# Attention into routed experts on one core: token rows by transposes, gate logits in column groups, another order of a pair's matmuls

## The chip, the cores and the metric

The kernel runs on one NeuronCore of a Trainium2 chip. The metric is the device time of one execution in microseconds (us), the median of three runs. A difference of 0.3% is 3.0 us.

## The reference

Three stages, all in float32. Attention with a sigmoid in place of the softmax, on 4 batches (b) of 12 heads, 448 tokens and head size 64; then a mixture of 8 experts, where each of the 1792 tokens goes to the expert with the largest gate logit; then a dense two-layer block. Cut to what matters:

```
scores = q @ k.T / 8 - log(448)
attn   = sigmoid(scores) @ v                 # [4, 12, 448, 64]
x      = attn as [1792 tokens, 768]
logits = x @ w_gate                          # [1792, 8]
e      = argmax(logits);  gate = softmax(logits)[e]
x      = gate * (relu(x @ w1[e]) @ w2[e])
out    = relu(x @ w_in)**2 @ w_out
```

The argmax makes the logits delicate: they are computed in full float32, where TensorE makes two passes of each matmul (two records in the trace).

## The kernel before, in words

The change lies in the attention stage, lines 130 to 289. It works through 24 units: a unit is a pair of heads, (b, j) with j from 0 to 5, so that the pair's 128 output features are the columns 128j to 128j+127 of x. The loop over units (from line 259) writes out by hand the order in which every engine gets its instructions; within one engine the order of the program is kept. It is a pipeline over units: in iteration n the scores of unit n are computed, the products with v of unit n-1, and the token rows of unit n-2.

TensorE's 128x128 array is used in three forms. In the **row form** the array is cut into two halves of 64 rows: `score` (L181) for c = 0, 1, 2 computes 128 keys of both heads side by side, one head in each half, as three passes of a split into a rounded and a rest part (L168, L169 on DVE make the parts). In the **column form** it is cut into halves of 64 columns: `av` (L191) for c = 0, 1, 2 multiplies v with the attention of both heads side by side. In the **full form** the whole array is used: `score` for c = 3 (L183, the last 64 keys of both heads), `av` for c = 3 (L194), and `rows` (L204).

In one iteration TensorE gets, in this order: score 0 and 1 of unit n (row form), av 0 and 1 of unit n-1 (column form), score 2 (row form), score 3, av 3 and rows (full form), av 2 (column form). Scores go through ACT (the sigmoid, L185) into tiles `a`. The four av steps of a unit accumulate in one bank `po`, and `fin_av` (L198, DVE) copies it to `xT`, features by tokens.

`rows` (L200 to 212) turns xT of a unit into token rows and also gives the unit's share of the gate logits: for each of four chunks of 112 tokens it multiplies xT (stationary) with `iw`, the identity of 128 columns beside the 8 gate columns of this j: 136 moving columns, two passes, 8 passes a unit. ACT copies the result to `xn` (L206), a DMA on ACT's queue writes the rows to `x_d`, and DVE adds the 8 logit columns to `lg` (L210, L212). After the last unit the routing begins with a maximum over `lg` on DVE (L335).

Beside this DVE and ACT convert the weights of the dense block, two iterations to a chunk of weights (`convert`, lines 226 to 243; its operations are L106, L108, L111, L113 on DVE and L109 on ACT). In an iteration DVE gets, in this order: the split of the unit after the next score (L168, L169), the first half of the conversion, the logits' add, the copy to xT, the second half of the conversion. So behind the copy to xT there stand, in DVE's queue, a conversion step of half the chunk and the split of the next iteration. SP's queue holds the loads of q, k, v (L160, L161) and of raw weights (L95); POOL's queue holds the writes of converted weights (L115, L125).

PSUM is full: two banks of `po`, two of `pt`, four of score tiles.

Of the kernel before, what the change touches and what calls it, by code (L numbers as in the profile page):

```python
# [10 lines left out]
F32 = mybir.dt.float32  # L11
# [5 lines left out]
AF = mybir.ActivationFunctionType  # L17
ALU = mybir.AluOpType
AX = mybir.AxisListType

B, H, S, D = 4, 12, 448, 64
NT = B * S
DM = H * D
E = 8
# [2 lines left out]
NP = H // 2  # L27
CP = 112
NC = S // CP
KD = DM // 128  # L30
KF = FF // 128
KF2 = FF2 // 128
NR = B * NC
IW = 128 + E
NTL = NT // 128
NSLOT = NTL + E - 1
NBASE = NTL + 1
# [24 lines left out]
def moe_kernel(ctx: ExitStack, tc: tile.TileContext, qk, v, wg, wm, w2, out):  # L62
    nc = tc.nc
# [6 lines left out]
    x_d = dram.tile([NT + 128, DM], F32, name="x_d")  # L70
# [5 lines left out]
    ident = const.tile([128, 128], F32, name="ident")  # L76
# [57 lines left out]
    with ExitStack() as actx:  # L134
        xp = actx.enter_context(tc.tile_pool(name="xp", bufs=1, reuse_waits="tile"))
        sp_ = actx.enter_context(tc.tile_pool(name="sp_", bufs=2, reuse_waits="tile"))
        ps_a = actx.enter_context(tc.tile_pool(name="ps_a", bufs=2, space=PS, reuse_waits="tile"))
        wctx = actx.enter_context(ExitStack())
        ps_e = actx.enter_context(tc.tile_pool(name="ps_e", bufs=1, space=PS, reuse_waits="tile"))
# [2 lines left out]
        ap_ = wctx.enter_context(tc.tile_pool(name="ap_", bufs=6, reuse_waits="tile"))  # L142

        xT = {}
        iw = xp.tile([128, KD, IW], F32, name="iw")
        lg = xp.tile([CP, NR, E], F32, name="lg")
        for j in range(KD):
            nc.gpsimd.tensor_copy(iw[:, j, :128], ident)
        zero = xp.tile([128, DM // 8], F32, name="zero")
        nc.gpsimd.memset(zero, 0.0)  # L150

# [12 lines left out]
        def split_qk(n):  # L164
            r = loaded[n][0]
            rh = sp_.tile([128, QW], F32R, tag="qkh", name=f"qkh{n}")
            rl = sp_.tile([128, QW], F32R, tag="qkl", name=f"qkl{n}")
            nc.vector.tensor_copy(rh, r)  # L168
            nc.vector.tensor_tensor(rl, r, f32(rh), op=ALU.subtract)  # L169
            return [(rh, rh), (rh, rl), (rl, rh)]  # L170

        def score(b, j, c, terms):
            ps = ps_s.tile([128, 2, 512], F32, tag="sc", name=f"sc_{b}_{j}_{c}")
            o = S + 128 * c
            n = 2 if c < 3 else 1
            for i, (kp, qp) in enumerate(terms):
                flags = dict(start=(i == 0), stop=(i == len(terms) - 1), skip_group_check=True)
                if c < 3:
                    for h in range(2):
                        p = slice(64 * h, 64 * h + 64)  # L180
                        nc.tensor.matmul(ps[:, h, :S], kp[p, o:o + 128], qp[p, :S], **flags)  # L181
                else:
                    nc.tensor.matmul(ps[:, 0, :S], kp[:, o:o + 128], qp[:, :S], **flags)  # L183
            a = ap_.tile([128, 2, S], F32, tag="a", name=f"a_{b}_{j}_{c}", bufs=9)
            nc.scalar.activation(a[:, :n], ps[:, :n, :S], AF.Sigmoid, bias=bias_s, scale=1.0 / math.sqrt(D))  # L185
            return a

        def av(b, j, c, a, vr, po):
            if c < 3:
                for h in range(2):  # L190
                    nc.tensor.matmul(po[64 * h:64 * h + 64, :S], vr[:, 128 * c + 64 * h:128 * c + 64 * h + 64], a[:, h],  # L191
                                     start=(c == 0), stop=(c == 2), skip_group_check=True)
            else:
                nc.tensor.matmul(po[:, :S], vr[:, 384:512], a[:, 0], start=False, stop=False, skip_group_check=True)  # L194

        def fin_av(b, j, po):
            xT[b, j] = xp.tile([128, S], F32, tag="xT", name=f"xT_{b}_{j}", bufs=3)
            nc.vector.tensor_copy(xT[b, j], po[:, :S])  # L198

        def rows(b, j):  # L200
            pt = ps_e.tile([128, 2, 512], F32, tag="pt", name=f"pt_{b}_{j}")
            xn = sp_.tile([128, NC, IW], F32, tag="xn", name=f"xn_{b}_{j}")
            for c in range(NC):
                nc.tensor.matmul(pt[:CP, c // 2, (c % 2) * IW:(c % 2) * IW + IW], xT[b, j][:, c * CP:(c + 1) * CP], iw[:, j, :],  # L204
                                 start=True, stop=True, skip_group_check=True)
            nc.scalar.activation(xn[:CP].rearrange("p (a c) n -> p a (c n)", a=2), pt[:CP, :, :2 * IW], AF.Copy)  # L206
            nc.scalar.dma_start(out=x_d[128 + b * S:128 + (b + 1) * S, j * 128:(j + 1) * 128].rearrange("(c p) d -> p c d", p=CP), in_=xn[:CP, :, :128])
            l = lg[:, b * NC:(b + 1) * NC, :]
            if j == 0:
                nc.vector.tensor_copy(l, xn[:CP, :, 128:])  # L210
            else:
                nc.vector.tensor_tensor(l, l, xn[:CP, :, 128:], op=ALU.add)  # L212

        units = [(b, j) for b in range(B) for j in range(NP)]
        loaded = {n: load(*units[n]) for n in range(3)}
        done = []
        rawb, raw = [], []

        def extras():
            rows(*done.pop(0))  # L220
# [5 lines left out]
        def convert(n, half):  # L226
            if n < 2:
                if half == 0:
                    fetch(n)
                return  # L230
            m, o = divmod(n - 2, 2)
            if m < 0 or m >= PRE:
                return
            if o == 0 and half == 0:
                conv[m] = (conv[m], cvp.tile([128, 2 * CH if m >= 8 else CH], F32, tag="dst", name=f"cd{m}"),
                           cvp.tile([128, CH], F32, tag="ab", name=f"ca{m}", bufs=1))
            narrow(m, 1 + 2 * o + half, *conv[m])
            if o == 1 and half == 0 and m + 2 < PRE:
                fetch(m + 2)
            if o and half:  # L240
                narrow(m, 5, *conv[m])
            if (m == PRE - 1 if o and half else o == 0 and half == 0 and m > 0):
                last = m if o else m - 1
                narrow(last, 6, *conv.pop(last))

        def fetch(m):
            conv[m] = cvp.tile([128, 2 * CH], F32, tag="src", name=f"cs{m}")
            narrow(m, 0, conv[m], None, None)

        def av_step(c):  # L250
            if prev is not None:
                b, j, parts_, vr, po = prev
                av(b, j, c, parts_[c], vr, po)
                if c == 2:
                    fin_av(b, j, po)
                    done.append((b, j))

        terms = {0: [(loaded[0][0], loaded[0][0])]}
        for n, (b, j) in enumerate(units):
            if n + 3 < len(units):  # L260
                loaded[n + 3] = load(*units[n + 3])
            if n == 0:
                nc.sync.dma_start(out=iw[:, :, 128:], in_=wg)
                nc.sync.dma_start(out=x_d[0:128, :].rearrange("p (a n) -> p a n", a=8), in_=zero.unsqueeze(1).to_broadcast([128, 8, DM // 8]))
            if n >= len(units) - 4:
                rawb.append(rawp.tile([128, 2 * CH], F32, tag="raw", name=f"raw{n}", bufs=4))
                raw.extend([rawb[-1][:, :CH], rawb[-1][:, CH:]])
            vr = loaded.pop(n)[1]
            if n + 1 < len(units):
                terms[n + 1] = split_qk(n + 1)  # L270
            r = terms.pop(n)
            po = ps_a.tile([128, 512], F32, tag="po", name=f"po_{b}_{j}")
            cur = [score(b, j, 0, r), score(b, j, 1, r)]
            av_step(0)
            av_step(1)
            convert(n, 0)
            cur.append(score(b, j, 2, r))
            cur.append(score(b, j, 3, r))
            av_step(3)
            if done:  # L280
                extras()
            av_step(2)
            convert(n, 1)
            prev = (b, j, cur, vr, po)
        extras()
        for c in (0, 1, 3, 2):
            av_step(c)
        extras()
        wctx.close()

# [16 lines left out]
        m, me, es, g, gr, pos = (rt([CP, NR], n) for n in ("m", "me", "es", "g", "gr", "pos"))  # L307
# [151 lines left out]
    def trans_y(bi, h, t, yn, yT, pool, tags):  # L459
# [5 lines left out]
        for i in range(2):  # L465
            pt = pool.tile([128, 4, 128], F32, tag=tags[i], name=f"pyt_{bi}_{h}_{t}_{i}")
            js = range(i * per, min(KD, (i + 1) * per))
            for j in js:
# [16 lines left out]
    with ExitStack() as mctx:  # L485
# [19 lines left out]
        def xtrans(s, xg):  # L505
            xh = mp.tile([128, KD, 128], F32R, tag="xh", name=f"xh_{s}", bufs=1)
            xl = mp.tile([128, KD, 128], F32R, tag="xl", name=f"xl_{s}", bufs=1)
            for i, (j0, n) in enumerate(((0, 4), (4, 2))):
# [34 lines left out]
        def make_slot(s, xh, xl, weights):  # L543
# [14 lines left out]
            def up(c):  # L558
# [4 lines left out]
                for q in range(3):  # L563
# [3 lines left out]
                    o = q * 512  # L567
                    mm3(ps[i], xh[:, k, :], xl[:, k, :], w[:, o:o + 512], wl_[:, o:o + 512], k == 0, k == KD - 1)
                if c % 2 == 1:
# [270 lines left out]
    for bi, (t0, P) in enumerate(blocks):  # L840
# [65 lines left out]
        po = {}  # L906
# [30 lines left out]
        for o in range(len(PRODS)):  # L937
            for q in range(4):
                g = 4 * o + q
# [24 lines left out]
                if ty and g >= 20 and g - 20 < len(ty):  # L964
                    i = g - 20
# [59 lines left out]
```

## Time and profile before

| | |
|---|---|
| median of 3 runs | 995.42 us (994.38 to 997.09) |
| profiled execution, its time | 997.18 us |
| profiled execution, its span | 995.7 us |
| TensorE (PE) busy | 948.8 us, 95% |
| DVE, ACT busy | 637.6 us, 565.8 us |
| mean granted clock of PE | 0.976 of full speed |
| attention stage | to about 186 us |

The span is from the first to the last instruction of the profiled execution. PE is its matmuls, PEld its weight loads. In a timeline, each row is a run of like instructions of one line; the time of the last one includes the way through the array, so that consecutive rows overlap a little, and the distance from one start to the next tells what a step costs. A bracket behind a row tells how long the engine was idle before it, and what ended that.

### The profile page before, as it was taken

The numbers are of one execution on the slowest core, as the hardware profiler recorded it, in microseconds if no ns is written. First come the engines' busy times: TensorE is split into PE (matmuls) and PEld (weight loads), VectorE is DVE, ScalarE is ACT, GpSimd is POOL, SyncE is SP. The second block draws the span as 40 slices with busy tenths as digits, with TensorE's granted clock in tenths as the row PEclk, the third lists the DMA queues.
The fourth block names the chain that finished last, engine by engine and source line by source line (L and its number), as shares of the span: only waits on it lengthen the run. The fifth ranks groups of instructions, "written<-read, shape, count | busy, mean of one in ns | idle before, by whom it ended". The sixth has DMA issues, their size and how long they took to land. (4 is left out here: it accounts for less than half of the span.)

```text
span 995.7 us, 15057 instructions
## 1 busy us (share of the span) xinstructions
PE 948.8 (95%) x5870; PEld 799.4 (80%) x5870; DVE 637.6 (64%) x671; ACT 565.8 (57%) x674; POOL 144.1 (14%) x120
## 2 busy tenths in 40 slices
PE   7999999458999999999998999999999999999996
PEld 3555555247888888888887888889999999999996
DVE  2777779678777776777764467617776722228763
ACT  5666666265777777777774544536544434446540
POOL 0000000145513233421330000000000110000002
PEclk9999999777999999999999999999999999999998
DMA  8798887552496876359465164443334541223412
GB/s 289 245 322 288 291 296 255 190 239 79 136 384 213 312 280 223 128 196 360 160 235 188 29 260 184 153 164 95 96 96 143 183 150 64 64 65 96 127 32 95
DMA packets 51261, 184.32 MB, mean 185 GB/s; under 512 B 7856, under 2 KB 18736, under 8 KB 49136
## 3 DMA queue, kind: packets, MB, share of 16 engines
q1 hardware_dynamic: 33136, 146.48, 42.0%
q0 software_dynamic: 6832, 31.07, 8.0%
q10 hardware_dynamic: 11216, 5.75, 2.3%
q8 instruction: 47, 0.77, 0.3%
q14 instruction: 30, 0.25, 0.1%
HBM read 209.62 MB, written 36.97 MB: 248 GB/s over the span
## 5 line engine op out<-in xcount | busy, mean ns | idle before, releaser
L397 DVE TENSOR_TENSOR wl<-raw,wh 128x1536 fp32r<-128x1536 f32 x103 | 203.2, 1981 | 70.1 <-ACT wh L396 67.3
L396 ACT ACTIVATE wh<-raw 128x1536 fp32r<-128x1536 f32 x120 | 177.8, 1488 | 14.3 <-DMA raw<-in_wm 6.9
L185 ACT ACTIVATE a<-sc,bias_s 128x896 f32<-128x896 f32 x96 | 82.4, 908 | 36.0 <-PE sc L181 35.7
L864 ACT ACTIVATE r<-pp 128x512 f32<-128x512 f32 (+1 forms) x64 | 34.8, 544 | 111.5 <-PE pp L860 111.5
L956 PE MATMUL pq<-wrh,sh 128*128 128x384 f32 x264 | 89.1, 337 | 0.3 <-DVE raw L917 0.3
L958 PE MATMUL pq<-wrh,sl 128*128 128x384 f32 x264 | 88.7, 336 | 0.0
L957 PE MATMUL pq<-wrl,sh 128*128 128x384 f32 x264 | 88.7, 336 | 0.0
L527 PE MATMUL py<-wl,hh 128*128 128x384 f32 x240 | 82.8, 345 | 5.5 <-POOL wl L397 5.5
L526 PE MATMUL py<-wh,hh 128*128 128x384 f32 x240 | 86.3, 360 | 0.0
L528 PE MATMUL py<-wh,hl 128*128 128x384 f32 x240 | 83.0, 346 | 2.5 <-DVE hl L556 2.5
L397 POOL TENSOR_TENSOR wl<-raw,wh 128x1536 fp32r<-128x1536 f32 x17 | 60.0, 3534 | 161.4 <-ACT wh L396 161.4
L526 PE MATMUL ph<-wh,xh 128*128 128x512 f32 x180 | 76.0, 422 | 0.3 <-ACT xh L512 0.3
L397 DVE TENSOR_TENSOR wrl<-raw,wrh 128x1536 fp32r<-128x1536 f32 x30 | 52.7, 1757 | 35.8 <-ACT wrh L396 35.8
L527 PE MATMUL ph<-wl,xh 128*128 128x512 f32 x180 | 71.8, 399 | 0.0
L396 ACT ACTIVATE wrh<-raw 128x1536 fp32r<-128x1536 f32 x30 | 44.6, 1487 | 47.8 <-PE pq L958 43.0
L528 PE MATMUL ph<-wh,xl 128*128 128x512 f32 x180 | 71.7, 399 | 0.0
L872 DVE TENSOR_TENSOR h<-h,h 128x512 f32<-128x512 f32 (+1 forms) x16 | 10.0, 625 | 89.9 <-ACT h L867 89.9
L885 DVE TENSOR_TENSOR sl<-h,sh 128x1024 fp32r<-128x1024 f32 (+1 forms) x56 | 59.8, 1085 | 8.5 <-ACT sh L884 8.4
L191 PE MATMUL po<-a,qkv 128*64 128x448 f32 x288 | 64.7, 556 | 0.0
L832 POOL DMA_INDIRECT out<-raw,idx x14 | 13.7, 976 | 331.5 <-DVE raw L917 302.8
L884 ACT ACTIVATE sh<-h 128x1024 fp32r<-128x1024 f32 (+1 forms) x56 | 51.5, 943 | 13.5 <-PE pq L957 8.0
L858 PE MATMUL pp<-why,wrh 128*128 128x512 f32 (+1 forms) x132 | 48.9, 370 | 3.0 <-PEq L788 3.0
(235 smaller groups left out, 2188.3 us busy)
## 6 DMA issues: line engine op xcount, KB each, us to landing
raw<-in_wm SPq DMA_DIRECT2D x120, 768.0 KB
qraw<-in_wm SPq DMA_DIRECT2D x32, 768.0 KB
raw<-t_d SPq DMA_DIRECT2D x28, 768.0 KB
cs<-in_w SPq DMA_DIRECT2D x11, 1536.0 KB
raw<-w_d SPq DMA_DIRECT2D x16, 768.0 KB
qkv<-in_qk SPq DMA_DIRECT2D x23, 480.0 KB
raw<-in_w SPq DMA_DIRECT2D x5, 1536.0 KB
t_d<-raw POOLq DMA_DIRECT2D x5, 1536.0 KB, 7.7
```

Of the source, the lines that this page charges most:

```text
L185: nc.scalar.activation(a[:, :n], ps[:, :n, :S], AF.Sigmoid, bias=bias_s, scale=1.0 / math.sqrt(D))
L191: nc.tensor.matmul(po[64 * h:64 * h + 64, :S], vr[:, 128 * c + 64 * h:128 * c + 64 * h + 64], a[:, h], start=(c == 0), stop=(c == 2), skip ...
L396: nc.scalar.activation(h, src, AF.Copy)
L397: (nc.gpsimd if pool else nc.vector).tensor_tensor(l, src, f32(h), op=ALU.subtract)
L526: nc.tensor.matmul(ps, lh, rh, start=first, stop=False)
L527: nc.tensor.matmul(ps, lh, rl, start=False, stop=False)
L528: nc.tensor.matmul(ps, ll, rh, start=False, stop=last)
L884: nc.scalar.activation(sh[:, :2 * N], src, AF.Copy)
L885: V.tensor_tensor(sl[:, :2 * N], src, f32(sh[:, :2 * N]), op=ALU.subtract)
L956: nc.tensor.matmul(po[p][:, :DH], lh, wc[:, w0:w0 + DH], start=(q == 0 and kk == 0 and o in (0, 2, 5)), stop=False, **fl)
L957: nc.tensor.matmul(po[p][:, :DH], lh, wcl[:, w0:w0 + DH], start=False, stop=False, **fl)
L958: nc.tensor.matmul(po[p][:, :DH], ll, wc[:, w0:w0 + DH], start=False, stop=(q == 3 and kk == 1), **fl)
```

## The change

Three things. First, `rows` no longer multiplies with the identity beside the gate columns but uses TensorE's transpose with the identity: four instructions of 128 moving columns, one pass each. `pt` shrinks to one bank. Second, the gate logits are computed apart, by a new function `logits`: when j is 2 or 5 it multiplies the gate columns of three units (8 columns padded with zeros to 32, stationary) with their xT (448 moving columns), each unit in a group of 32 columns of the array of its own, into the freed bank `lgT`. When j is 5, the sums of the batch are complete: DVE copies 96 partitions of 448 columns to `ls`, four small matmuls with `pick` (8 moving columns) add the three groups and turn them into token rows, and DVE copies these to `lg`. `logits` is called right after score 0 and 1, and three more tiles of xT must live so long (5 buffers instead of 3). Third, the order within an iteration: score 0 and 1 (row form), the logits where due (column groups of 32), av 0, 1 and 2 (column form), score 2 (row form), score 3, rows and av 3 (full form). At the end of the stage: the rows of the last unit but one, av 0 to 3, the logits, the rows of the last unit.

```diff
+GW = 32
+GJ = 3
-IW = 128 + E
...
-        iw = xp.tile([128, KD, IW], F32, name="iw")
+        gw = xp.tile([128, KD, GW], F32, name="gw")
+        pick = xp.tile([128, E], F32, name="pick")
         lg = xp.tile([CP, NR, E], F32, name="lg")
-        for j in range(KD):
-            nc.gpsimd.tensor_copy(iw[:, j, :128], ident)
+        nc.gpsimd.memset(gw, 0.0)
+        nc.gpsimd.tensor_tensor(pick, ident[:, 0:E], ident[:, GW:GW + E], op=ALU.add)
+        nc.gpsimd.tensor_tensor(pick, pick, ident[:, 2 * GW:2 * GW + E], op=ALU.add)
...
-            xT[b, j] = xp.tile([128, S], F32, tag="xT", name=f"xT_{b}_{j}", bufs=3)
+            xT[b, j] = xp.tile([128, S], F32, tag="xT", name=f"xT_{b}_{j}", bufs=5)
             nc.vector.tensor_copy(xT[b, j], po[:, :S])
+        lgT = {}
+        def logits(b, j):
+            if j % GJ < GJ - 1:
+                return
+            if j == GJ - 1:
+                lgT[b] = ps_e.tile([128, 512], F32, tag="lgT", name=f"lgT_{b}")
+            for g in range(GJ):
+                i = j + 1 - GJ + g
+                nc.tensor.matmul(lgT[b][GW * g:GW * g + GW, :S], gw[:, i, :], xT[b, i], start=(i == g), stop=(i != g),
+                                 skip_group_check=True, tile_position=(0, GW * g))
+            if j < KD - 1:
+                return
+            ls = xp.tile([128, S], F32, tag="ls", name=f"ls_{b}", bufs=1)
+            nc.vector.tensor_copy(ls[:GJ * GW], lgT[b][:GJ * GW, :S])
+            o = lgT[b][:CP, S:S + NC * E].rearrange("p (c e) -> p c e", c=NC)
+            for c in range(NC):
+                nc.tensor.matmul(o[:, c], ls[:GJ * GW, c * CP:(c + 1) * CP], pick[:GJ * GW], start=True, stop=True, skip_group_check=True)
+            nc.vector.tensor_copy(lg[:, b * NC:(b + 1) * NC, :], o)
         def rows(b, j):
-            pt = ps_e.tile([128, 2, 512], F32, tag="pt", name=f"pt_{b}_{j}")
-            xn = sp_.tile([128, NC, IW], F32, tag="xn", name=f"xn_{b}_{j}")
+            pt = ps_e.tile([128, NC, 128], F32, tag="pt", name=f"pt_{b}_{j}")
+            xn = sp_.tile([128, NC, 128], F32, tag="xn", name=f"xn_{b}_{j}")
             for c in range(NC):
-                nc.tensor.matmul(pt[:CP, c // 2, (c % 2) * IW:(c % 2) * IW + IW], xT[b, j][:, c * CP:(c + 1) * CP], iw[:, j, :],
-                                 start=True, stop=True, skip_group_check=True)
-            nc.scalar.activation(xn[:CP].rearrange("p (a c) n -> p a (c n)", a=2), pt[:CP, :, :2 * IW], AF.Copy)
+                nc.tensor.transpose(pt[:CP, c], xT[b, j][:, c * CP:(c + 1) * CP], ident)
+            nc.scalar.activation(xn[:CP], pt[:CP], AF.Copy)
-            l = lg[:, b * NC:(b + 1) * NC, :]
-            if j == 0:
-                nc.vector.tensor_copy(l, xn[:CP, :, 128:])
-            else:
-                nc.vector.tensor_tensor(l, l, xn[:CP, :, 128:], op=ALU.add)
...
             if n == 0:
-                nc.sync.dma_start(out=iw[:, :, 128:], in_=wg)
+                nc.sync.dma_start(out=gw[:, :, :E], in_=wg)
...
             cur = [score(b, j, 0, r), score(b, j, 1, r)]
+            if done:
+                logits(*done[0])
             av_step(0)
             av_step(1)
+            av_step(2)
             convert(n, 0)
             cur.append(score(b, j, 2, r))
             cur.append(score(b, j, 3, r))
-            av_step(3)
             if done:
                 extras()
-            av_step(2)
+            av_step(3)
             convert(n, 1)
             prev = (b, j, cur, vr, po)
         extras()
-        for c in (0, 1, 3, 2):
+        for c in range(4):
             av_step(c)
+        logits(*done[0])
         extras()
```

`extras` is the call of `rows` for the oldest finished unit. `av_step(3)` now calls `fin_av`, where `av_step(2)` did.

## Rows read from the trace of the kernel before

**Rows 1.** Page, granted clock of PE in 40 slices of the span, in tenths.

```profile
PEclk9999999777999999999999999999999999999998
```

**Rows 2.** Windows, attention: stretch, length, busy us by engine, granted clock, DMA share, GB/s.

```profile
100.00:150.00 50.00, 50.00 (x301) 28.62 (x297) 37.93 (x43) 32.93 (x39) 1.60 (x3) 1.00 0.84 291
```

**Rows 3.** Timeline of PE over one iteration: start us, us, line, tiles, count.

```profile
126.78 0.47 PE L181 MATMUL sc<-qkh 64*128 64x448 f32 x2
127.08 0.37 PE L181 MATMUL sc<-qkl,qkh 64*128 64x448 f32 x2
...
127.89 0.36 PE L181 MATMUL sc<-qkh,qkl 64*128 64x448 f32 x2
128.19 1.72 PE L191 MATMUL po<-a,qkv 128*64 128x448 f32 x8
129.84 0.48 PE L181 MATMUL sc<-qkh 64*128 64x448 f32 x2
...
131.36 0.91 PE L194 MATMUL po<-a,qkv 128*128 128x448 f32 x2
132.12 1.09 PE L204 MATMUL pt<-iw,xT 128*112 128x136 f32 x8
133.13 0.97 PE L191 MATMUL po<-a,qkv 128*64 128x448 f32 x4
134.04 0.47 PE L181 MATMUL sc<-qkh 64*128 64x448 f32 x2
```

**Rows 4.** Source line 204: count, shortest, median and longest of one in ns.

```profile
L204 PE MATMUL pt<-iw,xT x192: 279/279/341, 23.2 to 185.0; 128*112 128x136 f32 x192
```

**Rows 5.** Timeline of PE in the experts' stage, around four transposes.

```profile
270.23 0.60 PE L554 MATMUL pht<-ident,hr 128*128 128x128 f32 x4
270.58 0.48 PE L526 MATMUL ph<-wh,xh 128*128 128x512 f32 x1
270.90 0.40 PE L527 MATMUL ph<-wl,xh 128*128 128x512 f32 x1
271.13 0.40 PE L528 MATMUL ph<-wh,xl 128*128 128x512 f32 x1
```

**Rows 6.** Timeline of PE, matmuls in four groups of 32 columns.

```profile
263.74 0.86 PE L633 MATMUL qa<-qraw,qxT 128*32 128x128 f32 x24
264.54 0.50 PE L526 MATMUL ph<-wh,xh 128*128 128x512 f32 x1
```

**Rows 7.** Timeline of DVE in the iteration of rows 3.

```profile
126.89 0.62 DVE L198 COPY xT<-po 128x448 f32<-128x448 f32 x1
127.44 1.75 DVE L108 SCALAR_TENSOR_TENSOR cd<-cs,cd 128x1536 uint32<-128x1536 uint32 x1
...
130.86 1.75 DVE L111 SCALAR_TENSOR_TENSOR cd<-cs,cd 128x1536 uint32<-128x1536 uint32 x1
```

**Rows 8.** Timeline of PE at the end of the attention stage.

```profile
178.65 1.15 PE L204 MATMUL pt<-iw,xT 128*112 128x136 f32 x8 [0.82 <-DVE xT L198]
179.73 1.72 PE L191 MATMUL po<-a,qkv 128*64 128x448 f32 x8
...
184.12 1.15 PE L204 MATMUL pt<-iw,xT 128*112 128x136 f32 x8 [0.82 <-DVE xT L198]
```

**Rows 9.** Timeline of DVE there.

```profile
183.35 0.62 DVE L198 COPY xT<-po 128x448 f32<-128x448 f32 x1 [0.96 <-PE po L191]
...
186.19 0.29 DVE L335 TENSOR_REDUCE m<-lg 112x16 f32<-112x128 f32 x1
```

**Rows 10.** Windows around two gaps of PE (columns as in rows 2).

```profile
219.40:221.30 1.90, 0.01 (x1) 0.01 (x1) 1.87 (x1) 1.90 (x3) 1.83 (x1) 1.00 0.00 0
221.70:228.40 6.70, 5.32 (x19) 5.18 (x19) 6.59 (x10) 2.88 (x4) 0.57 (x1) 0.50 0.05 15
...
538.40:541.30 2.90, 0.00 (x0) 0.00 (x0) 0.28 (x1) 2.06 (x2) 0.00 (x0) 1.00 0.88 315
...
542.50:545.80 3.30, 3.30 (x10) 2.56 (x9) 0.34 (x2) 0.00 (x0) 0.57 (x1) 0.50 0.62 182
```

More of the change, by code (lines that the diff above doesn't have):

```diff
@@ L191, in av @@
                     nc.tensor.matmul(po[64 * h:64 * h + 64, :S], vr[:, 128 * c + 64 * h:128 * c + 64 * h + 64], a[:, h],
-                                     start=(c == 0), stop=(c == 2), skip_group_check=True)
+                                     start=(c == 0), stop=False, skip_group_check=True)
             else:
-                nc.tensor.matmul(po[:, :S], vr[:, 384:512], a[:, 0], start=False, stop=False, skip_group_check=True)
+                nc.tensor.matmul(po[:, :S], vr[:, 384:512], a[:, 0], start=False, stop=True, skip_group_check=True)
@@ L206, in rows @@
-            nc.scalar.activation(xn[:CP].rearrange("p (a c) n -> p a (c n)", a=2), pt[:CP, :, :2 * IW], AF.Copy)
-            nc.scalar.dma_start(out=x_d[128 + b * S:128 + (b + 1) * S, j * 128:(j + 1) * 128].rearrange("(c p) d -> p c d", p=CP), in_=xn[:CP, :, :128])
-            l = lg[:, b * NC:(b + 1) * NC, :]
-            if j == 0:
-                nc.vector.tensor_copy(l, xn[:CP, :, 128:])
-            else:
-                nc.vector.tensor_tensor(l, l, xn[:CP, :, 128:], op=ALU.add)
+                nc.tensor.transpose(pt[:CP, c], xT[b, j][:, c * CP:(c + 1) * CP], ident)
@@ L214, in moe_kernel @@
+            nc.scalar.activation(xn[:CP], pt[:CP], AF.Copy)
+            nc.scalar.dma_start(out=x_d[128 + b * S:128 + (b + 1) * S, j * 128:(j + 1) * 128].rearrange("(c p) d -> p c d", p=CP), in_=xn[:CP])
         units = [(b, j) for b in range(B) for j in range(NP)]
@@ L253, in av_step @@
                 av(b, j, c, parts_[c], vr, po)
-                if c == 2:
+                if c == 3:
                     fin_av(b, j, po)
```

## The prediction, made before the changed kernel ran

> **What bounds the kernel now.** The page first: PE is busy for 95% of the span, and its clock is full except in three slices of the experts' start [rows 1]. The change touches the attention stage alone, so the windows of that stage come next: from 100 to 150 us PE is busy for all 50 us, DVE for 38, ACT for 33, and DMA at a share of 0.84 [rows 2]. So in this stage PE's own stream sets the pace, and what the change saves or adds on PE counts in full, 22 times (iterations 2 to 23 have all three kinds of work). Then the timeline of one iteration [rows 3]. The same row comes back after 134.04 - 126.78 = 7.26 us, and the reader should look at distances from start to start: score 0 and 1 take 1.41, av 0 and 1 1.65, score 2 and 3 1.52, av 3 0.76, [rows 1].01, av 2 0.91.
>
> In these distances the price of a change of form can be seen. Inside score 0 and 1 a pair of passes follows the next after 0.20 us (127.08 to 127.89 is four steps), but the first takes 0.30 and the last before av 0.30. av 3, which follows and is followed by the full form, needs 0.76 for two passes, 0.38 each; av 2, the same number of steps between two changes of form, needs 0.91. So a change of form costs 0.05 to 0.10 on each side of it, some 0.15 for the changes into and out of av 2.
>
> **The change part by part.** *Rows as transposes.* Removed: 8 passes in 1.01 us [rows 3]. Added: 4 transposes. Four transposes with 128 moving columns take 0.35 us to the start of the next matmul, whose own step is 0.32 where 0.23 follows [rows 5]: 0.35 + 0.09 = 0.44. Of the 1.01 about 0.08 is the change of form behind it (8 steps of 0.116, from (1.09 - 0.28)/7 with 0.28 for one pass [rows 4], are 0.93). Ends: 0.35 if the slow next step is not paid, 0.5 if both sides are; I take 0.44, the row itself.
>
> *The order.* av 2 joins av 0 and 1: 0.76 instead of 0.91. The change behind rows goes (0.08), and av 3 now stands before the row form and pays 0.10 for leaving. The new iteration: 1.41 + (1.65 + 0.76) + 1.52 + 0.44 + (0.76 + 0.10) = 6.64. Saved: 0.62; ends 0.50 and 0.75. Times 22 this is 13.6, and iteration 1, without rows, saves 0.15: **-13.8 us** (ends -11.2 and -16.6).
>
> *The logits on PE.* Seven times in the loop (j = 2 and 5; the eighth is in the tail) three fp32 matmuls of 448 columns run in three column groups. That such groups run side by side is seen in [rows 6]: 24 passes of 128 columns last 0.80 us with both changes of form, against 24 x 0.107 = 2.6 in turn (0.107 a step in [rows 5]: (0.60 - 0.28)/3, with 0.28 for one as in [rows 4]). So two steps of 0.38 and 0.15 for the extra form: 0.91. No row shows a change from 32 to 64 columns; its price lies between nothing and 0.15, and I take the upper end, as every change of form in [rows 3] costs. The Trainium skill, TensorEngine Tiling (Array Packing), Tiling Modes, says that a change of mode drains the engine and a change of tile within a mode does not; by it the upper end holds, while the lower end would make the sum 1.0 smaller. Sum: 7 x 0.9 = **+6.3 us** (ends 5.3 and 7.4).
>
> *The wait it adds.* When j is 5 (iterations 7, 13 and 19 of the loop), PE needs the copy `ls` from DVE before the four small matmuls, and everything of PE's order behind them, av 0 to 2 first, waits with them. The copy is not free when PE asks for it. In DVE's order it stands behind the copy to xT, L108 (these iterations all follow an even one) and the split; its place is the one L111 has in [rows 7]. xT starts 0.11 us after score 0 (126.89 against 126.78), and L111 starts at 130.86, 4.08 after score 0. The copy has the size of the xT copy, 0.62, and from the end of an xT copy to PE's next matmul there are 184.12 - (183.35 + 0.62) = 0.15 us [rows 8, 9]. So PE can go on at 4.85 us after score 0, having finished score and logits at 1.41 + 0.90 = 2.31: it stands for 2.54 us. Then four small matmuls, 8 passes with 112 stationary and 8 moving columns. The nearest rows: the old rows' passes, 0.116 each with the same 112 stationary columns, 0.93 in all; or the passes of [rows 6], 0.033 each with 32 stationary columns, 0.27. I take the first, as the weights are of that size, and 0.1 for the change of form behind it. Loss: 3 x (2.54 + 1.03) = **+10.7 us** (ends 3 x 2.8 = 8.4 and 12). DVE itself has room: the logits' adds go, and L111, which now stands behind the wait for the small matmuls, is needed only an iteration later.
>
> *The clock after the wait.* 2.5 us without a matmul, then a microsecond of thin ones. In this trace PE's clock went down around gaps of that kind: a gap of 1.9 us was followed by 6.7 us at 0.50 of 2.4 GHz, that is 1.2 GHz, and one of 2.9 us by 3.3 us at 0.50, beginning about a microsecond after the matmuls had begun again [rows 10]. Gaps of 0.8 us did not do it: the eight passes after the one at 178.65 take 1.08, as in the middle of the stage [rows 3, 8]. Half speed for 3.3 us costs 1.65 where PE works all the time; part of it may lie in the wait, so I take 1.4 for each: **+4.2 us** (ends 0, and 3 x 6.7/2 = 10).
>
> *The tail.* Before, the maximum over lg starts 2.84 us after the last xT copy [rows 9]. Now rows of unit 22 take 0.64 less (1.08 to 0.44), av in one run 0.2 less; behind the xT copy come 0.77 to PE, 0.92 logits, 0.77 for `ls`, 1.1 small matmuls, 0.2 copy to lg: 3.8. Together 0.1 later (ends -0.5 and +0.8). The last x rows are written some 0.7 us later, but the gather that reads them waits for the routing anyway.
>
> *What costs nothing.* The smaller xn copy and the logits' adds on ACT and DVE: PE hides both engines [rows 2]. The zeros of `gw` and `pick` on POOL at the start replace six copies of identities there. Of SP's queue only the load into `gw` is moved behind the zeros; it stands behind the first loads of q, k, v. If the iterations get 8% shorter, DMA must move as much in less time: 0.84 x 7.26/6.64 = 0.92, still under 1, and the three long iterations give it time.
>
> **Sum.** -13.8 + 6.3 + 10.7 + 4.2 + 0.1 = +7.5 us. Against the profiled execution: 997.18 + 7.5 = 1004.7. It lies 1.76 above the median of its runs, so on the median's level: 995.42 + 7.5, rounded down to **1002.5 us** for what of the low clock falls into work that waits anyway.
>
> **The rivals.** *The clock holds through the waits.* Then the sum is +3.3: 998.7 us, at the border of what a measurement can tell (0.3%, 3.0 us). For it: in the wait score and logits have just run at full pace, and the small matmuls follow. Against it: the fall after 1.9 us [rows 10]. The Trainium skill, TensorE: Matmul & The Clock Gate, Why this matters for your kernels, only asks to avoid gaps longer than the one computed here; by that rule the clock holds and the time is this rival's. The row of the 1.9 us gap disagrees with it.
>
> *Not slower: DVE is there in time.* If the copy stood first in DVE's queue when PE reaches it, a wait would cost 0.15 + 0.62 + 0.15, and with small matmuls at 0.27 1.2 us in all, too short for the clock: -13.8 + 6.3 + 3.6 + 0.1 = -3.8, 991.6 us. It decides from the point where a wait costs, with clock, under (13.8 - 6.3 + 3.0)/3 = 3.5 us: above -3 the kernel is no longer slower by more than can be measured. For it: PE may come later to the logits than I think, if a score waits. Against it: L108 and the split, 3.4 us of DVE, stand between the two copies in the program's order [rows 7].
>
> *The low clock lasts twice as long*, as after 219.4 us [rows 10]: 3 x 3.3 instead of 4.2, +13.2, 1008.6 us. Against it: there PE had further gaps in the low stretch (5.32 busy of 6.7).
>
> *The column groups run in turn.* 6 x 0.38 + 0.15 = 2.4 instead of 0.9, eight times: +12 more, 1014.5 us. Against it: [rows 6].
>
> *The order brings nothing* (forms cost as much as before): 0.13 x 22 = 2.9 more, 1005.4 us, inside the range.
>
> **How the numbers follow.** Forecast 0.62 (with the last rival's 0.04 inside), clock holds 0.16, DVE in time 0.10, long low clock 0.08, groups in turn 0.04. The range goes from 996.5, which takes in the clock holding with a saving near its end, to 1008: left out are DVE in time, the groups in turn and most of the long low clock, 0.19 in all. Slower: 0.60 of the forecast, half of the clock holding and the last two rivals make 0.80, cut to 0.73, because a term of 14 us stands against one of 21 and each may be off by a fifth; faster 0.10; same 0.17.
>
> **What would show it.** In the profile after: an iteration without logits of about 6.64 us; four transposes some 0.107 apart; in iterations 7, 13 and 19 a gap of PE of about 2.4 us before the small matmuls that ends with DVE's copy `ls`; a granted clock below 1 in the attention stage; the experts' and dense stages as before, only shifted. The prediction is wrong if PE shows no gap there, if `ls` starts sooner than 4 us after score 0, or if the clock stays full.

## The result and the profile after

The changed kernel took 1006.85 us, the median of four runs (1003.37 to 1008.1), beside 995.38 us for the kernel before, also the median of four. The ratio is 1.0102, with an interval from 1.0085 to 1.0119: about 10 us slower (the two medians lie 11.5 us apart). The profiled execution took 1007.0 us, its span is 1005.5 us, 9.8 more than before. (In the prediction's list of distances in an iteration, the step of `rows` is 1.01 us; it stands there garbled.)

First the granted clock of the page, in 40 slices, beside [rows 1]: there are two new dips in the attention stage (slices 5 and 7), which ends in slice 8 as before; a third, in slice 3, is too short for a digit.

```profile
PEclk9999898958999999999999999999999999999999
```

An iteration without logits of a whole batch, in PE's timeline, answers to [rows 3]:

```profile
45.99 0.48 PE L184 MATMUL sc<-qkh 64*128 64x448 f32 x2
...
47.42 2.48 PE L194 MATMUL po<-a,qkv 128*64 128x448 f32 x12
49.83 0.47 PE L184 MATMUL sc<-qkh 64*128 64x448 f32 x2
...
51.34 0.60 PE L227 MATMUL pt<-ident,xT 128*112 128x128 f32 x4
51.77 0.92 PE L197 MATMUL po<-a,qkv 128*128 128x448 f32 x2
52.62 0.47 PE L184 MATMUL sc<-qkh 64*128 64x448 f32 x2
```

From 45.99 to 52.62 it takes 6.63 us, against 7.26 before. The four transposes take 0.43 to the start of av 3, and the three av steps of the column form 2.41 in one run. So 15 of the 22 iterations gained 0.63 each. The next iteration is the first of the three in which the logits of a batch are finished. PE, and DVE in the same stretch:

```profile
52.62 0.47 PE L184 MATMUL sc<-qkh 64*128 64x448 f32 x2
...
54.05 0.95 PE L212 MATMUL lgT<-xT,gw 128*32 128x448 f32 x6
57.46 0.92 PE L220 MATMUL lgT<-pick,ls 96*112 96x8 f32 x8 [2.46 <-DVE ls L217]
58.31 3.57 PE L194 MATMUL po<-a,qkv 128*64 128x448 f32 x12
61.81 0.74 PE L184 MATMUL sc<-qkh 64*128 64x448 f32 x2
...
65.13 0.47 PE L184 MATMUL sc<-qkh 64*128 64x448 f32 x2
```

```profile
52.73 0.62 DVE L201 COPY xT<-po 128x448 f32<-128x448 f32 x1 [1.71 <-PE po L197]
53.27 1.75 DVE L109 SCALAR_TENSOR_TENSOR cd<-cs,cd 128x1536 uint32<-128x1536 uint32 x1
54.94 0.66 DVE L171 CAST qkh<-qkv 128x960 fp32r<-128x960 f32 x1
55.63 1.16 DVE L172 TENSOR_TENSOR qkl<-qkv,qkh 128x960 fp32r<-128x960 f32 x1
56.70 0.61 DVE L217 COPY ls<-lgT 96x448 f32<-96x448 f32 x1
```

The reader should see the bracket behind the small matmuls: PE stood for 2.46 us, until DVE's copy `ls`. DVE was not idle in that time; it worked through a conversion step and the split that stand ahead of the copy, as in [rows 7], and began the copy 4.08 us after score 0. Then the av run, 2.48 us elsewhere, is 3.57 us long: its end runs at half clock. The iteration takes 12.51 us. The second such iteration is worse; PE's timeline again:

```profile
100.60 0.95 PE L212 MATMUL lgT<-xT,gw 128*32 128x448 f32 x6
103.92 1.66 PE L220 MATMUL lgT<-pick,ls 96*112 96x8 f32 x8 [2.37 <-DVE ls L217]
105.51 4.75 PE L194 MATMUL po<-a,qkv 128*64 128x448 f32 x12
110.19 0.71 PE L184 MATMUL sc<-qkh 64*128 64x448 f32 x2
...
113.24 0.47 PE L184 MATMUL sc<-qkh 64*128 64x448 f32 x2
```

Here the small matmuls take 1.59 us to the next start instead of 0.85, and av 4.68 instead of 2.41. The windows (columns as in [rows 2]) show why:

```profile
59.60:62.90 3.30, 3.30 (x14) 1.14 (x10) 0.68 (x1) 0.00 (x0) 0.00 (x0) 0.50 0.09 27
101.60:103.90 2.30, 0.00 (x0) 0.00 (x0) 2.23 (x3) 1.63 (x2) 0.00 (x0) 1.00 0.95 394
104.00:110.70 6.70, 6.70 (x22) 3.23 (x24) 1.86 (x2) 0.00 (x0) 0.00 (x0) 0.50 0.37 139
111.00:149.00 38.00, 38.00 (x229) 20.42 (x228) 27.66 (x27) 25.85 (x31) 1.60 (x3) 1.00 0.83 297
151.80:152.00 0.20, 0.00 (x0) 0.00 (x0) 0.15 (x1) 0.00 (x0) 0.00 (x0) 0.50 0.96 384
151.70:158.50 6.80, 6.49 (x22) 3.04 (x24) 2.11 (x3) 0.00 (x0) 0.00 (x0) 0.50 0.27 98
```

After the first wait the clock is at 0.50, that is 1.2 GHz, for 3.3 us, while PE is busy throughout; after the second for 6.7 us. Between the waits it is full, and PE has no gap. The third iteration:

```profile
147.26 0.47 PE L184 MATMUL sc<-qkh 64*128 64x448 f32 x2
...
152.01 1.66 PE L220 MATMUL lgT<-pick,ls 96*112 96x8 f32 x8 [2.37 <-DVE ls L217]
...
161.22 0.47 PE L184 MATMUL sc<-qkh 64*128 64x448 f32 x2
```

The third wait has a low stretch as long as the second's, but this one begins 0.3 us before the wait ends, some 2.1 us after PE had stopped and before any small matmul has run. The three iterations take 12.51, 14.06 and 13.96 us.

The end of the stage, on DVE, beside [rows 9]:

```profile
193.50 0.62 DVE L201 COPY xT<-po 128x448 f32<-128x448 f32 x1 [0.37 <-PE po L197]
...
197.04 0.29 DVE L355 TENSOR_REDUCE m<-lg 112x16 f32<-112x128 f32 x1
```

The maximum over lg starts at 197.04, 10.85 us later than before. The span grew by 9.8, so the experts' stage, with its own low stretches, gave back about one microsecond.

### The profile page after: what moved, and what is told of

It reads as the page before. It is cut to its first block, busy times and chain, and to the rows that moved or that the text cites. A ratio compares the mean times of both kernels' runs of the same rounds, so it can differ in the third digit from the quotient of the medians.

```text
span 1005.5 us, 15012 instructions
## 1 busy us (share of the span) xinstructions
PE 952.8 (95%) x5854; PEld 792.7 (79%) x5854; DVE 636.1 (63%) x655; ACT 562.8 (56%) x674; POOL 144.4 (14%) x117
```

## The experiments

Six kernels ran, one of them twice. Each is compared with runs of the kernel before on the same chip. The first three look for the cause of the loss; the order alone and the three runs behind it take the gain apart.

### The small matmuls later

```diff
             nc.vector.tensor_copy(ls[:GJ * GW], lgT[b][:GJ * GW, :S])
+            late.append((b, ls))
...
+        def finish():
+            if not late:
+                return
+            b, ls = late.pop()
             o = lgT[b][:CP, S:S + NC * E].rearrange("p (c e) -> p c e", c=NC)
...
             cur.append(score(b, j, 3, r))
+            finish()
             if done:
                 extras()
```

The four small matmuls and the copy to lg become a function of their own, called behind score 3; at the end of the stage it is called right after the logits.

> The four small matmuls and the copy to lg move behind score 3, ahead of rows; the copy to ls stays where it is in DVE's order. Theory (the loss is the wait for ls and the low clock that it brings): PE does not wait for ls any more, the three iterations with logits of a whole batch fall from 12.5 to 14.1 us to about 6.63 + 0.88 + 0.85 = 8.4, the clock stays full in the attention stage, and the time falls by some 15 us against the changed kernel, to about 991.5: below the kernel before. Rival (the thin small matmuls lower the clock, not the wait): low stretches stay behind them, and the time lies at 996 to 1001.

It took 990.31 us, a ratio of 0.9947 (0.9932 to 0.9962): faster than the kernel before, and 16.5 us below the changed kernel's median (15.4 us by the two ratios, each to the kernel before on its own chip). The first iteration that finishes a batch, on PE:

```profile
51.63 0.47 PE L184 MATMUL sc<-qkh 64*128 64x448 f32 x2
...
53.05 0.95 PE L212 MATMUL lgT<-xT,gw 128*32 128x448 f32 x6
53.94 2.48 PE L194 MATMUL po<-a,qkv 128*64 128x448 f32 x12
...
57.86 0.86 PE L228 MATMUL lgT<-pick,ls 96*112 96x8 f32 x8
58.58 0.63 PE L235 MATMUL pt<-ident,xT 128*112 128x128 f32 x4
...
59.88 0.47 PE L184 MATMUL sc<-qkh 64*128 64x448 f32 x2
```

8.25 us, with no gap ahead of the small matmuls. A window over most of the stage shows PE busy for all of it and the clock full, with the small matmuls inside it:

```profile
50.00:170.00 120.00, 120.00 (x724) 63.56 (x723) 94.83 (x98) 80.64 (x95) 5.02 (x8) 1.00 0.84 299
```

So the thin matmuls do not lower the clock by themselves; that rival falls. The third wait of the changed kernel says so too: there the clock fell before they began.

### The wait filled with idle work

```diff
+            for i in range(3):
+                nc.tensor.matmul(lgT[b][GJ * GW:, :S], gw[:, i, :], xT[b, i + 3], start=True, stop=True,
+                                 skip_group_check=True, tile_position=(0, GJ * GW))
             ls = xp.tile([128, S], F32, tag="ls", name=f"ls_{b}", bufs=1)
```

> Three matmuls of 448 columns that nobody reads (gate columns of three units again, in the fourth column group of lgT) stand between the logits and the small matmuls, about 2.3 us of PE work inside the wait of 2.4 us. Theory (wait and low clock are two prices, and the low clock comes from the idle time): DVE's copy comes no sooner, so the iterations keep the wait, 6.63 + 0.88 + 2.45 + 0.85 = 10.8 to 11 us each, but the clock stays full: 32.7 instead of 40.5 us in the three, about 999. Rival (the thin matmuls lower the clock): no gain, about 1006. Rival (the wait is nothing, all is the clock): about 992.

1000.77 us, a ratio of 1.0059 (1.0038 to 1.0080). On PE:

```profile
52.00 0.47 PE L184 MATMUL sc<-qkh 64*128 64x448 f32 x2
...
53.85 2.04 PE L217 MATMUL lgT<-xT,gw 128*32 128x448 f32 x5
56.84 0.92 PE L223 MATMUL lgT<-pick,ls 96*112 96x8 f32 x8 [0.95 <-DVE ls L220]
57.69 2.48 PE L194 MATMUL po<-a,qkv 128*64 128x448 f32 x12
...
62.90 0.47 PE L184 MATMUL sc<-qkh 64*128 64x448 f32 x2
```

The small matmuls start 4.84 us after score 0, as they did in the changed kernel (57.46 - 52.62). But the gap is 0.95 us, av takes 2.41 again, and the iteration 10.90; the other two take 10.86 and 10.83. From 50 to 180 us the granted clock is 1.00:

```profile
50.00:180.00 130.00, 127.34 (x752) 66.63 (x750) 95.21 (x98) 82.39 (x97) 5.01 (x8) 1.00 0.78 281
```

Work that nobody reads made the kernel faster, by 6.1 us between the medians and by 4.3 us by the two ratios, whose intervals do not meet. Neither rival came, 1006 or 992. So the loss has two parts: the wait itself, which is still there, 10.90 against 8.25 us, and the low clock, which the idle time brought: 12.51, 14.06 and 13.96 against 10.90, 10.86 and 10.83, together 7.9 us in the profiled executions.

### The split behind the logits

```diff
-            if n + 1 < len(units):
-                terms[n + 1] = split_qk(n + 1)
             r = terms.pop(n)
...
                 logits(*done[0])
+            if n + 1 < len(units):
+                terms[n + 1] = split_qk(n + 1)
             av_step(0)
```

> The changed kernel with the split of the next unit behind the logits in DVE's order, so that ls comes 1.76 us sooner. Theory (the length of DVE's queue ahead of ls sets the wait): the gap of PE falls from 2.4 to about 0.7 us, too short for the clock; the three iterations take about 6.63 + 0.88 + 0.65 + 0.9 = 9.1 us, about 993.5 in all. Rival (ls waits for something else, the bank or the matmuls' end): the gap stays, about 1006.

992.78 us, a ratio of 0.9966 (0.9955 to 0.9978). The copy and the small matmuls:

```profile
54.89 0.92 PE L220 MATMUL lgT<-pick,ls 96*112 96x8 f32 x8 [0.85 <-DVE ls L217]
```

```profile
52.31 1.75 DVE L109 SCALAR_TENSOR_TENSOR cd<-cs,cd 128x1536 uint32<-128x1536 uint32 x1
54.12 0.62 DVE L217 COPY ls<-lgT 96x448 f32<-96x448 f32 x1
```

The copy follows the conversion step at once, the gap shrinks by 1.6 us to 0.85 (0.76 in the other two iterations), and the clock stays full until the end of the stage. The length of DVE's queue ahead of the copy sets the wait; the rival, that the copy waits for the bank or for the matmuls, falls.

### The order alone, in the kernel before

```diff
             av_step(1)
+            av_step(2)
             convert(n, 0)
...
-            av_step(3)
             if done:
                 extras()
-            av_step(2)
+            av_step(3)
```

Beside this, as in the change, the copy to xT follows av 3, and the accumulation ends there.

> The kernel before with the new order alone: av 0, 1, 2 in one run, then score 2, 3, rows (still the matmul with identity and gate columns, with its adds on DVE), av 3. Theory (a change of form costs PE's own time): one excursion into the column form less, 0.13 to 0.15 us in each of 22 iterations, an iteration of 7.12, about 992.3. Rival (the order alone brings nothing, as PE's weight loads or a wait for scores take its place): 995.4, an iteration of 7.26.

992.96 us, 3.3 us below the kernel before beside it (996.22), a ratio of 0.9970 (0.9958 to 0.9981). An iteration:

```profile
124.85 0.47 PE L181 MATMUL sc<-qkh 64*128 64x448 f32 x2
...
130.19 1.09 PE L204 MATMUL pt<-iw,xT 128*112 128x136 f32 x8
131.11 0.92 PE L194 MATMUL po<-a,qkv 128*128 128x448 f32 x2
131.95 0.47 PE L181 MATMUL sc<-qkh 64*128 64x448 f32 x2
```

7.10 us instead of 7.26, and rows to av 3 takes 0.92, without the 0.09 of a change of form behind it. The rival, 7.26, falls.

### One part undone in the faster kernel

Two kernels start from the one with the small matmuls late; that one ran again beside them. The first goes back to the old order:

```diff
             av_step(1)
-            av_step(2)
             convert(n, 0)
...
+            av_step(3)
             finish()
             if done:
                 extras()
-            av_step(3)
+            av_step(2)
```

In it the copy to xT follows av 2 again, and the accumulation ends there.

> The kernel with the small matmuls late, but with the old order: av 0 and 1, score 2 and 3, av 3, small matmuls, rows, av 2. Theory: one more excursion into the column form, 0.14 us in each of 22 iterations, 6.77 instead of 6.63 us, 3 us more than with the new order, about 993.3. Rival (once rows are short the order is worth nothing): 990.3.

The second computes rows as plain matmuls:

```diff
-                nc.tensor.transpose(pt[:CP, c], xT[b, j][:, c * CP:(c + 1) * CP], ident)
+                nc.tensor.matmul(pt[:CP, c], xT[b, j][:, c * CP:(c + 1) * CP], ident, start=True, stop=True, skip_group_check=True)
```

> The kernel with the small matmuls late, but with rows as plain matmuls by the identity, two passes of 128 columns for each of four chunks, in place of four transposes. Theory: 8 x 0.109 = 0.87 instead of 0.44 us, an iteration of 7.06 instead of 6.63 us, 22 x 0.43 = 9.5 us more, about 999.8. Rival (the transposes saved less, and the order more, than they were put at): an iteration of 6.85, about 995.

> The kernel with the small matmuls late once more, beside the two that undo one part of it on the same chip: about 0.9947 of the kernel before, iterations of 6.63 us.

| kernel | us | ratio to before (interval) | iteration without logits, us |
|---|---|---|---|
| small matmuls late, again | 990.81 | 0.9935 (0.9919 to 0.9952) | 6.62 |
| old order | 993.85 | 0.9977 (0.9967 to 0.9988) | 6.78 |
| rows as plain matmuls | 1000.25 | 1.0036 (1.0022 to 1.0050) | 7.05 |

PE with the old order, then with plain matmuls:

```profile
104.89 0.47 PE L184 MATMUL sc<-qkh 64*128 64x448 f32 x2
...
111.67 0.47 PE L184 MATMUL sc<-qkh 64*128 64x448 f32 x2
```

```profile
107.73 0.47 PE L184 MATMUL sc<-qkh 64*128 64x448 f32 x2
...
113.06 1.03 PE L235 MATMUL pt<-ident,xT 128*112 128x128 f32 x8
113.94 0.92 PE L197 MATMUL po<-a,qkv 128*128 128x448 f32 x2
114.78 0.47 PE L184 MATMUL sc<-qkh 64*128 64x448 f32 x2
```

The order is worth 3.0 us (993.85 - 990.81), the transposes 9.4 us (1000.25 - 990.81). Spread over 22 iterations these are 0.14 and 0.43 us; the timelines have 0.16 and 0.43. Neither rival came. The last kernel also shows what the logits cost once they stand apart: without the transposes their price would not be paid back, and it is slower than the kernel before.

## Why the prediction was right, and which term was too small

The forecast was 1002.5 us in a range from 996.5 to 1008.0, slower; measured were 1006.85. The mechanism was the one forecast, step by step; one term, the low clock, was too small by nearly half. The table sets its terms beside the two profiled executions.

| term | predicted, us | in the profile after |
|---|---|---|
| transposes and order | -13.8 | 22 x (7.26 - 6.63) = -13.9 |
| logits in column groups, 7 times | +6.3 | 0.88 each, +6.2 |
| wait for `ls` and small matmuls, 3 times | +10.7 | 32.59 - 3 x (6.63 + 0.88) = +10.1 |
| low clock behind the waits | +4.2 | 40.53 - 32.59 = +7.9 |
| end of the stage | +0.1 | 7.56 - 7.54 = 0.0 |

The second row is the length of the iterations that only add three units' logits, 7.51 us, less 6.63. In the third, 32.59 is the sum of the three iterations with the filled wait, taken as the price without the low clock; in the fourth, 40.53 is that of the three in the changed kernel. The last row goes from the start of the rows of unit 22 to the maximum over lg.

**Transposes and order.** Predicted 6.64 us, measured 6.63. The rows of transposes in another stage [rows 5] gave the right step, 0.44 against 0.43, and the kernels that undo one part split the gain about as the sum did: 0.16 for the order, put at 0.13, and 0.43 for the transposes, put at 0.49 (the matmuls that stand in for them there have 128 moving columns, not 136). Iteration 1, put at 0.15, gained nothing (6.33 us before, 6.35 after).

**The column groups.** Three groups run side by side: in the kernel with the small matmuls late six passes take 0.89 us to the next start (53.05 to 53.94), so the rival that they run in turn is out. For the change from 32 to 64 columns the price lies near the upper end, 0.15: if the passes are two steps of 0.38, as in av 3, 0.88 each leaves 0.12. That agrees with the Trainium skill, TensorEngine Tiling (Array Packing), Tiling Modes, by which every change of mode drains the engine.

**The wait.** Predicted 2.54 us, measured 2.46, 2.37 and 2.37; the copy began 4.08 us after score 0, as read off the place of another operation in DVE's queue [rows 7]. The eight thin passes take 0.85 at full clock, near the upper bound of 0.93: the row with the same 112 stationary columns was the right neighbour.

**The low clock** is the term that was mis-sized. It was put at 1.4 us for each wait, from one low stretch of 3.3 us, with part of it in the wait. The first wait cost 1.6 that way. The second and third brought 6.7 us at half clock, in which PE was busy throughout but for the last 0.3 us of the third wait, and cost 3.2 and 3.1. This was the rival "the low clock lasts twice as long", set aside because the long stretch of [rows 10] had further gaps in it; after these waits there were none, and it lasted as long. Two of the three waits went that rival's way, and the time measured lies nearer to its 1008.6 us than to the forecast. That it stayed in the range is in part luck: a long stretch after the first wait, too, would have added 1.6 us, which makes an estimated 1008.4. Nor did the stretches begin where the prediction put them, about a microsecond after the matmuls had begun again: the first began some 2.1 us after that, the second with them, the third 0.3 us ahead of them.

The other rival, that the clock holds, did not come: three gaps of 2.37 to 2.46 us brought three low stretches. It was the one by the rule of the Trainium skill, TensorE: Matmul & The Clock Gate, Why this matters for your kernels; the rows speak against that rule as a safe bound. After gaps of 0.76 to 0.95 us with the same thin matmuls behind them the clock did not fall.

**The rest.** At the beginning of the stage the profiled execution lost another 0.7 us: the second unit's scores start at 12.25 instead of 11.55. That is probably not the change's doing: the order alone, without `gw`, has 12.06, and the kernel with the small matmuls late has 11.23 in one profiled execution and 11.86 in the other. What moves this start was not tried. With it the terms make 11.0, and the marker at the stage's end moved by 10.85.

What stayed open: why the low stretch of a wait is sometimes short and sometimes twice as long, and what decides where it begins. The four runs of the changed kernel spread by 4.7 us, about what three short stretches cost, which would fit a number of stretches that changes from run to run. But the 23 runs of the kernel before beside the first experiments spread by 4.9 us, and only one run of the changed kernel was read in its trace, so this is not shown.

## What to carry to other kernels

A saving on the engine that sets the pace is kept only if nothing in its own order waits for a slower queue: before a copy by another engine is put between two matmuls, count what stands ahead of that copy in that engine's queue, and put the matmul that needs it as much later as the count says. Here moving four small matmuls behind some four microseconds of other matmuls turned a kernel 10 us slower into one 5 us faster, at the same work. Where TensorE must wait, the wait is not the whole price; the clock behind it can cost as much again, and here even useless matmuls in the gap paid.

## What was not expected of the hardware

After a gap of 2.37 us the granted clock stayed at 0.50 for 6.7 us although PE was busy in all of them, whereas after one of 2.46 us it was 3.3 us. In the third wait it fell while PE still stood, some 2.1 us after the last matmul. Matmuls that nobody reads, which cut the gap from 2.46 to 0.95 us, kept the clock at 1.00 and saved 7.9 us in the three iterations of the stage. And 8 passes of only 8 moving columns take 0.85 us, hardly less than the 0.92 of 8 passes with 136 moving columns in the kernel with the order alone: with 112 stationary columns the moving ones scarcely count up to there.
